# A spectral layer and a gated feed-forward on one core: three first-stage buffers, another order in the opening and on VectorE, half of each table mirrored by GpSimd

## The chip, the core and the metric

The kernel runs on one core of a Trainium2 chip. The core has a matrix engine (TensorE, PE in the profile, with its weight loads as PEld), VectorE (DVE), ScalarE (ACT), GpSimd (POOL) and SyncE (SP), which here issues every DMA. Matrix products land in PSUM, from which VectorE and ScalarE take them; everything else lies in SBUF or in DRAM. The metric is the device time of one execution in microseconds, lower is better. Three executions of the kernel before took 1774.48, 1773.59 and 1771.73 us: median 1773.59 us.

## The reference

```python
# x: 8 x 3136 x 256
X = np.fft.rfft(x, axis=1)
Yr = Xr @ w_r - Xi @ w_i + b_r
Yi = Xr @ w_i + Xi @ w_r + b_i
Yr = np.sign(Yr) * np.maximum(np.abs(Yr) - 0.01, 0.0)   # and Yi in the same way
y = np.fft.irfft(Yr + 1j * Yi, n=3136, axis=1)
h = np.maximum(y @ w_in, 0.0)                            # w_in: 256 x 1024
conv_out = sum(conv_w[k] * (h, shifted by k - 1 rows) for k in range(3))
return (h * sigmoid(conv_out)) @ w_out                   # w_out: 1024 x 256
```

A real Fourier transform along the sequence, a complex 256 × 256 mixing of the features, a soft threshold, the inverse transform, and then a feed-forward layer gated by a convolution of three taps. The feed-forward weights come as float64.

## The kernel before

**The transforms.** 3136 is 49 × 64, and each transform is two rounds of matrix products. Stage one (`stage1`, and `stage1_head` for batch 0) takes 49-point transforms with the constant `f1`; its results go through DRAM (`sc1`), because the second round needs them in another order. Stage two (`stage2`) loads them as `a2` and multiplies them by a table `t2`, one 128 × 128 matrix for each of 25 frequencies `u`. The result is split into a high part `fh` and a low part `fl` for products in the faster fp32r format; `mix` multiplies by the split weights `wmix_hi` and `wmix_lo` with three products in place of four (so there is a difference `d` of real and imaginary part as a third operand), `threshold` applies the soft threshold and splits again (`sh`, `sl`), and `stage3` multiplies by the inverse table, also split (`i1_hi`, `i1_lo`), and stores to DRAM (`sc2`). `stage4`, `up` and `down` are the second half: last round of the inverse transform, and the feed-forward in 28 chunks.

**Items.** Stages two, mixing, threshold and three run over 50 items: eight batches by six groups of four frequencies, and two items that gather the frequency left over. They are software-pipelined in the loop of line 430: in turn `it`, TensorE does stage two of item `it`, mixing of item `it - 1` and stage three of item `it - 3`; the threshold of item `it - 2` runs on ScalarE, VectorE and GpSimd. Between these, stage one of batches 1 to 7 is worked off in halves of a tile (`one`), by a plan of how many are due (`due`, line 434): 2 in turn 0, 3 in turn 1, 4 in turns 2 and 3, 3 in turn 4, later 3 and then 2.6 a turn until they are used up at turn 40. Each half is a product into the single PSUM buffer `ps_s1`, copied by ScalarE to `a1` (two buffers, line 254); each full tile is stored to `sc1`. `load_a2` of a new batch has to wait for all of that batch's stores.

**Order.** In the loop the instruction order of TensorE, VectorE and ScalarE is the order of the program: `some(g, n)` advances a stage by n steps, and the calls of lines 454 to 477 are the hand-written order of one turn. On VectorE that gives, in a turn: difference and low part of the first half of stage two (L306, L307), the threshold (L347, which needs ScalarE's L346 first), two conversion steps, difference and low part of the second half, mixing with bias (L333), the table split (L146, only in early turns), a conversion step, the low part of the difference (L311), and the last additions of the mixing (L337, four of them). ScalarE copies `sh` (L349) right after L347, and GpSimd then makes `sl` (L350), which has one buffer. The conversion steps (`back`, from turn 7) turn the float64 weights into two fp32r parts. SP and GpSimd have no hand-written order; a planner sorts their instructions by readiness, and `tc.issue_after(x)` forbids that what stands in its block is issued ahead of x.

**Tables.** `t2` is loaded in seven slices, slice g holding four frequencies, all 128 rows; the inverse table in seven slices to `raw` buffers (two, shared with the mixing weights), then split by ScalarE and VectorE (`split`, L145 and L146). For all but the frequency left over, rows 64 to 127 of each table are rows 0 to 63 with sine and cosine exchanged and some signs changed.

**The opening** (lines 384 to 418): `f1`, all of batch 0's input, stage one of batch 0 with its eight stores; then, after the last of these, the mixing weights, table slice 0, the first stage-one tile of batch 1 with its two halves, the first `a2`, biases, the second `a2`, two more tiles, and then the loop.

Of the kernel before, what the change touches and what calls it, by code (L numbers as in the profile page):

```python
# [101 lines left out]
def spectral_ffn_kernel(ctx: ExitStack, tc: tile.TileContext, x, w_r, w_i, b_r, b_i,  # L102
# [15 lines left out]
    small = cst.tile([P, 32], F32, name="small")  # L118
    mlam, warm = small[:, 0:1], small[:, 1:2]


    with ExitStack() as ab:
# [28 lines left out]
        def load_t2(g):  # L151
            sl = slice(g * UG, min((g + 1) * UG, U + 1))
            return nc.sync.dma_start(t2[:, sl, :], fwd2v[:, sl, :])

# [16 lines left out]
        def load_inv1(g):  # L171
            sl = slice(g * UG, min((g + 1) * UG, U + 2))
            raw = stg.tile([K2, sl.stop - sl.start, KQ], F32, name="i1_raw", tag="raw", bufs=2)
            nc.sync.dma_start(raw, inv1v[:, sl, :])
            return i1_hi[:, sl, :], i1_lo[:, sl, :], raw
# [76 lines left out]
        def stage1(b, jc, xr):  # L252

            a1 = s1p.tile([K1, JC, D], F32, name="a1", bufs=2)
            for j in range(0, JC, 2):
# [86 lines left out]
        def threshold(v):  # L342
            sh = wk.tile([K2, UG, D], F32R, name="sh")
            sl = wk.tile([K2, UG, D], F32R, name="sl", bufs=1)
            r = wk.tile([K2, UG, D], F32, name="r", bufs=1)
            nc.scalar.activation(r, v, AF.Relu, bias=mlam)  # L346
            nc.vector.scalar_tensor_tensor(v, v, LAM, r, op0=ALU.add, op1=ALU.min)  # L347
            yield sh, sl
            nc.scalar.copy(sh, v)  # L349
            SL_ENG.tensor_tensor(sl, v, sh.bitcast(F32), op=ALU.subtract)  # L350
            yield None
# [21 lines left out]
        nc.vector.memset(mlam, -LAM)  # L373
        nc.vector.memset(warm, 0.0)
        nc.scalar.activation(warm, warm, AF.Sigmoid)

# [8 lines left out]
        with tc.tile_pool(name="hx", bufs=1, reuse_waits="tile") as hx:  # L385
            xh = []
            for p in range(NQ):
                xr, ld = load_x(hx, 0, p, parts=2 if p == 0 else 1, tag=f"hx{p}")
                xh.append(xr)
            with tc.issue_after(ld.ins):  # L390
                st = stage1_head(xh)
        asked = []
# [11 lines left out]
        with tc.issue_after(st.ins):  # L404
            ld = load_mix()
        with tc.issue_after(ld.ins):
            ld = load_t2(0)
        ab.enter_context(tc.manual_schedule(engines={mybir.EngineType.PE}))
        with tc.issue_after(ld.ins):
            ask()  # L410
            some(first, 2)
            a2s[0], ld = load_a2(*items[0])
        with tc.issue_after(ld.ins):
            load_bias()
            a2s[1], ld = load_a2(*items[1])
            for _ in range(2):
                ask()
        ab.enter_context(tc.issue_after(ld.ins))
        wkf, wk, cab, io = [ab.enter_context(tc.tile_pool(name=nm, bufs=n, reuse_waits="tile"))
# [6 lines left out]
        background = later()  # L426
        given, held = 2, []
        xs, vs, ss, i1s = {}, {}, {}, {}
        ab.enter_context(tc.manual_schedule(engines={mybir.EngineType.DVE, mybir.EngineType.Activation}))
        for it in range(n_it + 3):  # L430
# [4 lines left out]
            n_a, given = due - given, due  # L435
            work = 3 if WP0 <= it < n_it else 0

            def one(k=0):
                some(first, n_a > k)
# [6 lines left out]
            if it <= NG:  # L446
                with tc.issue_after(ld.ins) if it + 2 < NG else ExitStack():
# [5 lines left out]
                    i1s[it] = load_inv1(it)  # L453
            some(two, 1)
            th = threshold(vs.pop(it - 2)[0]) if 0 <= it - 2 < n_it else iter(())
            ss[it - 2] = next(th, None)
            back(2)
            some(two, 1)
            some(mx, 8)
            one(1)  # L460
            some(th, 1)
            some(two, 1)
            some(mx, 5)
            if it - 1 in i1s:
                split(*i1s.pop(it - 1))
            back(1)
            some(two, 1)
            some(mx, 5 if n_a > 3 else 9)
            one(2)
            some(mx, 9)  # L470
            one(3)
# [156 lines left out]
```

## Time and profile before

| | |
|---|---|
| the three timed executions, median | 1773.59 us |
| the profiled execution, its own time | 1775.9 us |
| its span, from the first to the last instruction | 1774.1 us |
| mean granted TensorE clock | 0.987 |
| busy: TensorE, weight loads | 1730.7 us (98%), 1608.3 us (91%) |
| busy: VectorE, ScalarE, GpSimd | 1487.7 us (84%), 1209.1 us (68%), 118.5 us (7%) |
| moved by DMA | 165.47 MB |

The profile shows one execution; times in its rows count from the span's start. In a row of a timeline or of groups stand the engine, the line of the kernel, the operation and "tile written <- tiles read" with the shape; "xN" counts instructions that were merged; square brackets give the idle time of the engine before the row and what ended it. Durations of neighbouring instructions overlap on TensorE and, by some 0.1 us, on VectorE, so times from start to start are the better measure of pace. The chain of waits is followed back from the last instruction; its rows give a start, a length and the engine or transfer that held the chain then. "SPq" is SP's queue of DMA issues. PEclk is the granted TensorE clock as a share of full speed, and the DMA share is the mean busy share of the core's 16 DMA engines.

### The profile page before, as it was taken

The page shows a single profiled execution, that of the slowest core. Times are in us where ns is not written, and L with a number is a line of the kernel's source. Part 1 is how long each engine was busy: PE and PEld are TensorE (multiplying, and loading weights), DVE is VectorE, ACT ScalarE, POOL GpSimd, SP SyncE. Part 2 cuts the span into 40 slices and gives each one's busy share as a digit, 9 for nine tenths or more (in the row PEclk, how much of TensorE's full clock was granted, in tenths as well). Part 3 has the DMA queues.
Part 4 walks back from the last instruction along what each step waited for, and adds up shares of the span by engine and source line. Part 5 has one row for each costly group of instructions (what it writes and reads, how often), then busy time and mean ns, then how long its engine had stood idle before and what let it go on. Part 6 is the DMA issues. An engine that isn't in the chain of part 4 may idle for free.

```text
span 1774.1 us, 28820 instructions
## 1 busy us (share of the span) xinstructions
PE 1730.7 (98%) x11872; PEld 1608.3 (91%) x11872; DVE 1487.7 (84%) x1757; ACT 1209.1 (68%) x1565; POOL 118.5 (7%) x54
## 2 busy tenths in 40 slices
PE   6999999999888999999999999999999999999999
PEld 2788888888888999999999999999999999999998
DVE  2778898898994988888888888888888888888887
ACT  2567677677554777777777777777777777777766
POOL 0122222222221000000000000000000000000000
PEclk8999999999988999999999999999999999999999
DMA  8777677666424110111111111111101111100001
GB/s 249 223 236 243 213 230 251 219 224 217 127 93 129 38 40 22 38 46 46 50 48 47 46 40 49 50 40 50 49 21 40 49 50 40 49 22 21 22 21 42
DMA packets 108304, 165.47 MB, mean 93 GB/s; under 512 B 8492, under 2 KB 86316, under 8 KB 108174
## 3 DMA queue, kind: packets, MB, share of 16 engines
q1 hardware_dynamic: 108174, 163.64, 29.1%
q8 instruction: 94, 1.54, 0.3%
q14 instruction: 36, 0.29, 0.0%
HBM read 86.02 MB, written 77.59 MB: 92 GB/s over the span
## 4 chain that ended last, share of the span: by engine, by line
PE 92%; DVE 3%; DMA 3%; issue 1%; ACT 1%; SPq 0%; POOL 0%; ACTq 0%
PE acc L557 31%; PE ps_h L529 31%; PE ps_mx L329 9%; PE ps_s L510 7%; PE ps_s L257 5%; PE ps_s L301 4%; PE ps_s L360 3%; DVE v L337 1%; DMA sc<-a 1%; DMA t<-in_fwd_dram 1%; PE ps_s1h L274 1%; ACT r L346 1%; DMA xr<-in_x_dram 0%; DMA z<-sc 0%; DVE p L333 0%
## 5 line engine op out<-in xcount | busy, mean ns | idle before, releaser
L557 PE MATMUL acc<-wout,gh 128*128 128x256 f32 x3136 | 567.4, 280 | 0.0
L529 PE MATMUL ps_h<-yh,win 128*128 128x450 f32 x1792 | 550.1, 368 | 0.0
L538 DVE SCALAR_TENSOR_TENSOR c<-h,cw,c 128x896 f32<-128x896 f32 x448 | 513.5, 1148 | 38.9 <-ACT c L536 37.3
L557 PEld LDWEIGHTS acc<-wout,gh 128*128 128x128 f32 x3136 | 490.1, 188 | 5.1
L557 PE MATMUL acc<-wout,gl 128*128 128x256 f32 x1568 | 437.4, 280 | 0.0
L531 ACT ACTIVATE h<-ps_h 128x900 f32<-128x900 f32 x224 | 207.4, 926 | 260.4 <-PE ps_h L529 260.4
L529 PEld LDWEIGHTS ps_h<-yh,win 128*128 128x128 f32 x1792 | 339.0, 189 | 26.1 <-DVE yl L517 0.4
L529 PE MATMUL ps_h<-yl,win 128*128 128x450 f32 x896 | 329.4, 368 | 0.0
L544 DVE TENSOR_TENSOR gl<-c,gh 128x896 fp32r<-128x896 f32 x224 | 243.2, 1089 | 76.1 <-ACT gh L543 74.6
L557 PEld LDWEIGHTS acc<-wout,gl 128*128 128x128 f32 x1568 | 293.8, 188 | 0.6
L540 DVE TENSOR_TENSOR c<-h,c 128x896 f32<-128x896 f32 x224 | 243.4, 1087 | 48.1 <-ACT c L539 48.1
L543 ACT CAST gh<-c 128x896 fp32r<-128x896 f32 x224 | 211.1, 943 | 70.3 <-DVE c L540 68.3
L539 ACT ACTIVATE c<-c 128x896 f32<-128x896 f32 x224 | 213.0, 951 | 8.3 <-DVE c L538 4.5
L329 PE MATMUL ps_mx<-wmix_hi,fl 128*128 128x256 f32 x600 | 188.0, 313 | 7.6 <-DVE fl L311 7.6
L329 PE MATMUL ps_mx<-wmix_hi,fh 128*128 128x256 f32 x600 | 185.5, 309 | 1.8 <-DVE p L333 1.5
L529 PEld LDWEIGHTS ps_h<-yl,win 128*128 128x128 f32 x896 | 169.3, 189 | 10.9
L536 ACT ACTIVATE c<-h,cw 128x896 f32<-128x896 f32 x168 | 176.1, 1048 | 2.2 <-DVE gl L544 0.2
L329 PE MATMUL ps_mx<-wmix_lo,fh 128*128 128x256 f32 x600 | 171.1, 285 | 0.0
L350 POOL TENSOR_TENSOR sl<-v,sh 128x1024 fp32r<-128x1024 f32 x50 | 118.3, 2366 | 423.3 <-PE ps_s L360 321.6
L337 DVE TENSOR_TENSOR v<-ps_mx,p 64x512 f32<-64x512 f32 x200 | 137.5, 687 | 7.7 <-PE ps_mx L329 4.8
L329 PEld LDWEIGHTS ps_mx<-wmix_hi,fl 128*128 128x128 f32 x600 | 115.5, 192 | 21.1 <-issue 12.0
L510 PEld LDWEIGHTS ps_s<-i,z 100*128 100x128 f32 x1024 | 130.4, 202 | 4.6 <-DVE yl L517 2.2
(84 smaller groups left out, 1963.6 us busy)
## 6 DMA issues: line engine op xcount, KB each, us to landing
z<-sc SPq DMA_DIRECT2D x64, 400.0 KB
xr<-in_x_dram SPq DMA_DIRECT2D x63, 392.0 KB
a<-sc SPq DMA_DIRECT2D x48, 512.0 KB
sc<-z SPq DMA_DIRECT2D x48, 512.0 KB
out_dram<-o SPq DMA_DIRECT2D x27, 896.0 KB
sc<-a SPq DMA_DIRECT2D x56, 392.0 KB
sc<-ha SPq DMA_DIRECT2D x8, 392.0 KB
win_bits<-in_moe_w_in_dram SPq DMA_DIRECT2D x4, 512.0 KB
```

The source lines that it names most:

```text
L329: nc.tensor.matmul(ps[c][:, k, :], lt, rh, start=(n == 0), stop=(n == len(mm) - 1))
L337: nc.vector.tensor_tensor(v[dst, :, k, :], ps[c][src], p1[src, c], op=ALU.add)
L510: nc.tensor.matmul(ps[:, t, j * K1:(j + 1) * K1], z2[:, j, t * P:(t + 1) * P], i2, start=(j == 0), stop=(j == JG - 1), skip_group_check=True)
L529: nc.tensor.matmul(ps[:, a, 0:CH + 2], lt, rh, start=(n == 0), stop=(n == len(mm) - 1))
L531: nc.scalar.activation(h, ps[:, :, 0:CH + 2], AF.Relu)
L536: nc.scalar.mul(c, h[:, :, 0:CH], cw[:, 0, f:f + 1])
L538: nc.vector.scalar_tensor_tensor(c, h[:, :, k:k + CH], cw[:, k, f:f + 1], c, op0=ALU.mult, op1=ALU.add)
L539: nc.scalar.activation(c, c, AF.Sigmoid)
L540: nc.vector.tensor_tensor(c, h[:, :, 1:CH + 1], c, op=ALU.mult)
L543: nc.scalar.copy(gh, c)
L544: nc.vector.tensor_tensor(gl, c, gh.bitcast(F32), op=ALU.subtract)
L557: nc.tensor.matmul(acc[m // 2][:, m % 2, :], lt[:, sl], rh[:, f, :], start=(f == 0 and n == 0 and m % 2 == 0), stop=(f == NF - 1 and n == ...
```

## The change

Five edits come together.

- `a1`, the stage-one tile, gets three buffers.
- For all but slice 0 of `t2` and the last slice of the inverse table, only rows 0 to 63 are loaded. GpSimd makes rows 64 to 127 from them, by products with a constant +1 or -1 (`mirror_t2`) or with a column of the new tile `sign` that holds +1 or -1 for each group of 32 rows (`load_inv1`): four products for each slice of each table.
- In the opening, the mixing weights and table slice 0 are asked for behind the input of batch 0 and thus ahead of the head's stores; the first `a2` comes right after the last of these stores; the first stage-one tile of batch 1 comes after that `a2`, and its two halves run in turn 0, behind stage two (`given` starts at 0).
- In a turn, both halves of stage two come first; the threshold is cut into three steps, and each comes later: L346 after eight matmuls of the mixing, L347 after L333, `sh` and `sl` after the second stage-one half.
- The conversion steps run from turn 5, still three a turn, spread over the turn.

```diff
-    mlam, warm = small[:, 0:1], small[:, 1:2]
+    mlam, warm, sign = small[:, 0:1], small[:, 1:2], small[:, 2:4]
...
         def load_t2(g):
             sl = slice(g * UG, min((g + 1) * UG, U + 1))
-            return nc.sync.dma_start(t2[:, sl, :], fwd2v[:, sl, :])
+            rows = slice(0, KQ if g == 0 else R2)
+            return nc.sync.dma_start(t2[rows, sl, :], fwd2v[rows, sl, :])
+
+        def mirror_t2(g):
+            top, low = [t2[q, g * UG:(g + 1) * UG, :].rearrange("p u (c h m) -> p c h u m", c=2, h=2) for q in (slice(0, R2), slice(R2, KQ))]
+            for c in range(2):
+                for h in range(2):
+                    nc.gpsimd.tensor_scalar_mul(low[:, c, h], top[:, 1 - c, h], -1.0 if c == h else 1.0)
...
-            nc.sync.dma_start(raw, inv1v[:, sl, :])
+            rows = slice(0, SP if g < NG else K2)
+            nc.sync.dma_start(raw[rows], inv1v[rows, sl, :])
+            if g < NG:
+                top, low = [raw[q].rearrange("p (k o) (m c) -> p o c k m", o=2, c=2) for q in (slice(0, SP), slice(SP, K2))]
+                for o in range(2):
+                    for c in range(2):
+                        nc.gpsimd.tensor_scalar_mul(low[:, o, c], top[:, o, 1 - c], sign[SP:K2, (o + c + 1) % 2:(o + c + 1) % 2 + 1])
...
-            a1 = s1p.tile([K1, JC, D], F32, name="a1", bufs=2)
+            a1 = s1p.tile([K1, JC, D], F32, name="a1", bufs=3)
...
             nc.scalar.activation(r, v, AF.Relu, bias=mlam)
+            yield sh, sl
             nc.vector.scalar_tensor_tensor(v, v, LAM, r, op0=ALU.add, op1=ALU.min)
-            yield sh, sl
+            yield None
...
+        for k in range(4):
+            for c in range(2):
+                nc.vector.memset(sign[k * 32:(k + 1) * 32, c:c + 1], 1.0 if k % 2 == c else -1.0)
...
             with tc.issue_after(ld.ins):
+                load_mix()
+                load_t2(0)
                 st = stage1_head(xh)
...
         with tc.issue_after(st.ins):
-            ld = load_mix()
-        with tc.issue_after(ld.ins):
-            ld = load_t2(0)
-        ab.enter_context(tc.manual_schedule(engines={mybir.EngineType.PE}))
+            a2s[0], ld = load_a2(*items[0])
         with tc.issue_after(ld.ins):
             ask()
-            some(first, 2)
-            a2s[0], ld = load_a2(*items[0])
-        with tc.issue_after(ld.ins):
             load_bias()
             a2s[1], ld = load_a2(*items[1])
             for _ in range(2):
                 ask()
+        ab.enter_context(tc.manual_schedule(engines={mybir.EngineType.PE}))
...
-        given, held = 2, []
+        given, held = 0, []
...
-            work = 3 if WP0 <= it < n_it else 0
+            work = 5 <= it < n_it
...
-            some(two, 1)
+            if 0 < it + 1 < NG:
+                mirror_t2(it + 1)
+            some(two, 2)
             th = threshold(vs.pop(it - 2)[0]) if 0 <= it - 2 < n_it else iter(())
+            some(mx, 8)
+            back(1)
             ss[it - 2] = next(th, None)
-            back(2)
-            some(two, 1)
-            some(mx, 8)
             one(1)
-            some(th, 1)
             some(two, 1)
             some(mx, 5)
             if it - 1 in i1s:
                 split(*i1s.pop(it - 1))
             back(1)
+            some(th, 1)
             some(two, 1)
+            back(1)
             some(mx, 5 if n_a > 3 else 9)
             one(2)
+            some(th, 1)
             some(mx, 9)
             one(3)
             some(mx, 64)
```

## The prediction

> **What bounds the kernel now.** First the busy table by stretches of the span, cut where the work changes: head of stage one, the first items, the repeating middle, the last items, the passage to the second half, the second half.
>
> ```profile
> core 0: us, PE busy (x) PEld busy (x) DVE busy (x) ACT busy (x) POOL busy (x), PEclk, DMA share, GB/s
> 0.00:34.00 34.00, 18.97 (x33) 6.72 (x34) 8.30 (x14) 7.53 (x13) 0.20 (x4) 0.90 0.82 245
> 34.00:62.00 28.00, 22.17 (x123) 16.57 (x122) 18.41 (x29) 14.05 (x27) 2.37 (x1) 0.87 0.97 267
> 62.00:102.00 40.00, 37.72 (x232) 29.96 (x233) 26.71 (x42) 24.02 (x40) 7.07 (x3) 0.92 0.60 191
> 102.00:441.00 339.00, 339.00 (x2424) 291.70 (x2423) 300.83 (x493) 241.50 (x390) 80.76 (x35) 1.00 0.72 231
> 441.00:536.00 95.00, 82.62 (x625) 78.22 (x623) 89.23 (x134) 53.49 (x81) 24.43 (x11) 0.95 0.34 107
> ...
> 569.00:1774.10 1205.10, 1200.83 (x8256) 1156.33 (x8255) 1033.63 (x1033) 855.69 (x1005) 0.00 (x0) 1.00 0.13 40
> ```
>
> Three regimes. From 102 to 441 us and after 569 us TensorE is busy throughout at clock 1.00: a reordering of other engines buys nothing there. From 0 to 102 us TensorE idles, with the DMA engines at 82 to 97% at first. From 441 to 536 us VectorE is the fullest (89.23 of 95), and TensorE waits. The change acts on the second and third regimes alone. Next, the chain of waits of the opening:
>
> ```profile
> 24.10 4.86 DMA sc<-ha
> ...
> 32.37 10.85 DMA t<-in_fwd_dram
> ...
> 43.35 2.02 PE ps_s L301 x16
> ...
> 53.69 8.00 DMA sc<-a
> ...
> 79.98 1.79 PE ps_s L301 x16
> ...
> 101.45 2.02 PE ps_s L301 x16
> ```
>
> The last store of the stage-one head lands at 28.96; item 1 waits for its table slice until 43.22; a store issued at 53.69 holds the chain for 8.00 us. TensorE's and ScalarE's timelines say what that store does:
>
> ```profile
> 4.17 3.70 PE L274 MATMUL ps_s1h<-xr,f 98*98 98x512 f32 x4 [4.17 <-DMA xr<-in_x_dram]
> ...
> 33.72 2.00 PE L257 MATMUL ps_s<-xr,f 98*98 98x512 f32 x2 [10.42 <-DMA xr<-in_x_dram]
> ...
> 38.21 3.35 PE L301 MATMUL ps_s<-t,a 128*128 128x128 f32 x16
> ...
> 52.02 1.95 PE L301 MATMUL ps_s<-t,a 128*128 128x128 f32 x16
> ...
> 61.77 0.59 ACT L258 COPY a<-ps_s 98x512 f32<-98x512 f32 x1 [3.31 <-DMA sc<-a]
> 62.41 2.02 PE L257 MATMUL ps_s<-xr,f 98*98 98x512 f32 x2 [3.79 <-ACT a L258]
> ...
> 68.28 1.92 PE L301 MATMUL ps_s<-t,a 128*128 128x128 f32 x15
> ```
>
> Stage two (L301) of items 0, 1, 2, 3, 4 and 6 starts at 38.21, 43.35, 52.02, 68.28, 79.98 and 101.45. In item 2, ScalarE cannot evict a stage-one half, because both `a1` buffers await their stores; `ps_s1` has one buffer, so TensorE stands 3.79 us and comes back slow (two L257 passes in 2.02 us; 0.86 when warm, below).
>
> For the end of the loop, one item on VectorE, its start-to-start times, and what GpSimd does meanwhile:
>
> ```profile
> 510.47 0.42 DVE L306 TENSOR_TENSOR d<-ps_s,d 128x256 f32<-128x256 f32 x1
> 510.81 0.68 DVE L307 TENSOR_TENSOR fl<-ps_s,fh 128x512 fp32r<-128x512 f32 x1
> 511.66 1.23 DVE L347 SCALAR_TENSOR_TENSOR v<-v,r 128x1024 f32<-128x1024 f32 x1 [0.17 <-ACT r L346]
> 512.80 0.42 DVE L306 TENSOR_TENSOR d<-ps_s,d 128x256 f32<-128x256 f32 x1
> 513.13 0.68 DVE L307 TENSOR_TENSOR fl<-ps_s,fh 128x512 fp32r<-128x512 f32 x1
> 513.73 1.28 DVE L333 TENSOR_TENSOR p<-ps_mx,bias 128x512 f32<-128x512 f32 x2
> 514.92 2.14 DVE L311 TENSOR_TENSOR fl<-d,fh 128x512 fp32r<-128x512 f32 x1
> 516.99 2.80 DVE L337 TENSOR_TENSOR v<-ps_mx,p 64x512 f32<-64x512 f32 x4
> ...
> 519.84 0.42 DVE L306 TENSOR_TENSOR d<-ps_s,d 128x256 f32<-128x256 f32 x1
> ...
> 514.15 2.36 POOL L350 TENSOR_TENSOR sl<-v,sh 128x1024 fp32r<-128x1024 f32 x1 [6.99 <-ACT sh L349]
> ```
>
> An item takes 9.37 us with VectorE never free. L311 lasts 2.14 us; its median over all items is below. It begins behind GpSimd's `sl` (514.15 to 516.51) and ends 0.55 us after it: it is held until GpSimd is done. The Trainium skill, "SBUF — State Buffer", § Who interferes with whom, says that GpSimd and a VectorE instruction with two SBUF inputs exclude each other for a whole instruction; by that rule, the trace agrees (L311 reads `d` and `fh` from SBUF).
>
> **The change, part by part.** More rows, of prices: warm matmuls from the chain, L311's normal size, GpSimd's work, a transposed split held up early, and where the last rows lie.
>
> ```profile
> 155.18 3.27 PE ps_mx L329 x28
> ...
> 440.52 0.86 PE ps_s L257 x2
> L311 DVE TENSOR_TENSOR fl<-d,fh x50: 679/685/2397, 43.6 to 524.3; 128x512 fp32r<-128x512 f32 x50
> L350 POOL TENSOR_TENSOR sl<-v,sh 128x1024 fp32r<-128x1024 f32 x50 | 118.3, 2366 | 423.3 <-PE ps_s L360 321.6 <-ACT sh L349 101.7
> L613 POOL MEMSET const-float32-1.0<- 128x1 f32 x1 | 0.1, 99 | 0.0
> 58.49 1.92 DVE L146 TENSOR_TENSOR i_lo<-i_raw,i_hi 128x512 fp32r<-128x512 f32 x1
> 443.21 0.42 DVE L306 TENSOR_TENSOR d<-ps_s,d 128x256 f32<-128x256 f32 x1 [1.92 <-ACT fh L305]
> ...
> 445.40 0.69 DVE L196 SCALAR_TENSOR_TENSOR wout_e<-wout_bits,wout_e 128x512 int32<-128x512 int32 x1
> ...
> 504.16 0.69 DVE L210 TENSOR_TENSOR wout<-wout_m,wout_rest 128x512 fp32r<-128x512 f32 x1
> ...
> 532.88 2.80 DVE L337 TENSOR_TENSOR v<-ps_mx,p 64x512 f32<-64x512 f32 x4
> ```
>
> *The opening's new order.* SP's queue moves mixing weights and table slice 0 (768 KB) ahead of the head's stores, and the first stage-one tile behind the first `a2` load. The transfers run as a line: between 33.72 and 43.22 landed `a2` 512, biases 256, `a2` 512, two `xr` 784, slice 256: 2320 KB in 9.5 us, 244 KB/us. The head's last store then lands later by 0 (the 768 KB fit into the unused 18%) to 3.1 us (768/244); I take 1, so 30.0. Formerly `xr` and weights moved while that landing was awaited; now the line is empty and starts again. The very first `xr`, 196 KB, serves a matmul at 4.17; less 0.8 of transfer that bounds a start at 3.4 us, SP's own first microsecond included; I take 2. Then `a2` 512, `xr` 392, biases 256, `a2` 512, `xr` 784 and half a slice, 128: 2584 KB, 10.6 us: 42.6. Item 0 starts near 34 instead of 38.21, but its two halves follow it instead of preceding it, so nothing is won by item 1. What was hidden, the weights' five VectorE and three ScalarE instructions, goes between head evictions, where VectorE is busy 8.30 of 34 us; uncovered they cost some 3 us. The eight MEMSETs of `sign` lie under the wait for the first `xr`, until 4.17.
>
> *GpSimd's multiplies.* Four per slice of each table, 64 partitions by 128 elements. No row shows one. From below 0.10 (MEMSET of one element), from above 2.37 (`sl`, 1024 elements, two inputs). I take 0.4: an eighth of `sl` is 0.30, plus the MEMSET's 0.10. Item 1's slice needs its own four, and perhaps the inverse table's four ahead of them: 44.2 to 45.8; **45.0**, 1.65 us later than now. Afterwards both tables' multiplies work one item ahead; queued behind them on GpSimd is `sl`, used an item later, with 6.2 us to spare (an item's 10.0, worked out below, less 1.41 of stage three and 2.37).
>
> *Half tables.* Five slices save 128 KB each, the last 32, six inverse slices 128 each: 1.44 MB, 5.9 us of the line in all. Of this, what lies ahead of the 53.69 store brings it some 4 us earlier; from item 3 on transfers are hidden anyway (share 0.60). Counted inside the next step only.
>
> *Three `a1` buffers.* Item 2's wait goes. An item's work on TensorE: stage two 1.79 (16 matmuls), mixing 36 × 0.117 (3.27/28) = 4.21, a half 0.86, stage three 12 × 0.117 = 1.41. An item with three halves and all stages is thus 10.0. Item 1 keeps its 8.67; item 2, four halves: 9.44 in place of 16.26; item 3, four halves and stage three: 10.85 for 11.70; items 4 and 5 keep 21.47. From 45.0: 53.7, 63.1, 74.0, 95.4 against 101.45. What is late next is item 2's fifth tile, now earlier through the half tables. **Opening: −6 us**; bounds: +3.5 (item 1 at its latest, 3.1 us of stores besides, item 2 gaining 1 us) and −9.
>
> *Middle.* VectorE's sum is unchanged and fits; `sl` starts after stage three as before, beside L337, which reads PSUM. Items 5 and 6 start the weight conversions two items sooner; VectorE's free 1.7 us of an early item (10.0 less 8.3) hide them, and uncovered they cost under 2 us. **0**, ±1.
>
> *VectorE's order at the end.* The differences of both halves come first, then L333, L347, L311, L337; the `sh` copy and `sl` follow L347, so `sl` falls beside L337 instead of L311, and L347 no longer waits for ScalarE. An item: 0.34+0.60+0.33+0.60+1.19+1.14+0.60+2.83 = 7.63 us, TensorE's 7.41 (no halves) below it. Now: 443.21 to 535.68 is 92.5 us for items 41 to 49 and the last mix. Then: 9 × 7.63 = 68.7 us, the last mix's L333, L347, L337 5.2, and conversions. Of these, 14 instructions of some 0.55 us run between 445.40 and 504.77, 7.7 us; the first four fall into items 41 and 42, so a shift by two items leaves ten, 5.5 us. Sum 79.4, that is −13.1. Each new wait between two such nearly equal engines costs something; at 0.2 us an item, **−11**. Bounds: 0 (VectorE then waits for mixing as long as it now waits for GpSimd) and −15, TensorE also keeping its clock (0.95 now).
>
> The sum is −17 us: 1775.9, the profiled execution (span 1774.1 and 1.8 around it), becomes 1758.9. The median of the three runs lies 2.3 below the profiled one: **1756.6 us**.
>
> **Rivals.**
>
> *The multiplies hold VectorE* (17%). While eight of 0.4 us run, 3.2 us an item, instructions with two SBUF inputs stand, as L146 does above (1.92 us; a normal one 0.69). VectorE's early item, 7.63 and 0.69 for the split, becomes 11.5 against TensorE's 10: 1.5 us in five items, 7 in all, which uses up the opening's gain. For it: that row. Against: each multiply is short, and half of VectorE's item reads PSUM. Time: 1773.6 − 11 + 1 = 1764. The rule of the Trainium skill cited above, from "SBUF — State Buffer", speaks for this rival; it gives the same price.
>
> *The end gains nothing* (13%). `sl` starts later within the item; should stage three wait for it, TensorE is late in place of VectorE. Against: it has most of an item to spare. Time: 1773.6 − 6 = 1767.6.
>
> *GpSimd becomes the bound, slower* (9%). In five early items it does eight multiplies and one `sl`. It overruns an item's 10.0 us once a multiply exceeds 0.95 us; the loss, 5 × (8c + 2.37 − 10.0), equals the 17 us won at c = 1.38 us. At `sl`'s own 2.37 us, five items lose 57: 1813 us. For it: nothing here prices so short an instruction, and its operands are strided. Against: GpSimd's idle time, 423 us, and `sl` with eight times the elements.
>
> *It does not do what it says* (6%): the opening stays bound by the line of transfers, `a1` merely waits elsewhere, and the end is limited by TensorE's clock: within 2 us of 1773.6.
>
> **How the numbers follow.** The forecast has 55%. The range runs from 1748 (both gains at their ends, 9 and 15, and the middle's 1) to 1769 (one gain alone, at −6 with 1.4 for the middle), and leaves out the last two rivals and stray ends. A measurement here tells 0.2%, 3.5 us, from no change. Faster: forecast, first two rivals, less some overlap, 82%. Same: the last rival and the first two at their bounds, 9%. Slower: 9%.
>
> **What would show it.** Right: item 3's stage two starts near 63; no ScalarE copy L258 waits for `sc<-a` in item 2; items 42 to 49 follow each other at 8.0 to 8.5 us, with L311 (then further down in the file) at 0.7 and `sl` beside L337; multiplies of 0.3 to 0.5 us. Wrong: multiplies of over 1 us, item 1 after 47, a stage two that waits for GpSimd, L347 or L311 stretched to 2 us, or a middle longer than the present 340 us between item 6 and item 41.

## The result, and the profile after

| | before | after |
|---|---|---|
| median of five executions | 1773.59 us (1771.73 to 1775.54) | 1760.88 us (1759.1 to 1766.73) |
| the profiled execution, its own time | 1775.9 us | 1766.73 us |
| its span | 1774.1 us | 1765.0 us |

The ratio is 0.9932, interval 0.9913 to 0.9951: 12.7 us faster. That lies inside the range and 4 us above the forecast of 1756.6 us. The profiled execution of the changed kernel is the slowest of its five, so its span shows 9.1 us of gain where the medians show 12.7.

First three of the stretches of the span that were shown before, for the changed kernel (start and end, us, busy us and instructions on TensorE, its weight loads, VectorE, ScalarE, GpSimd, then the granted clock, the DMA share and GB/s):

```profile
34.00:62.00 28.00, 18.43 (x92) 14.96 (x93) 10.03 (x17) 8.30 (x18) 11.74 (x20) 0.70 0.98 210
...
102.00:441.00 339.00, 337.34 (x2397) 290.00 (x2396) 294.15 (x490) 239.94 (x388) 82.72 (x35) 0.99 0.72 233
441.00:536.00 95.00, 90.09 (x713) 86.67 (x712) 87.46 (x141) 59.52 (x88) 27.59 (x12) 0.96 0.38 123
```

From 34 to 62 us TensorE does 92 matmuls where it did 123, while the DMA engines are as busy as before (0.98) and move less (210 GB/s for 267). From 441 to 536 us it does 713 for 625. The middle is nearly full (337.34 of 339.00; before, 339.00). So the opening lost and the end won. The chain of waits of the changed kernel, cut to the first 110 us (start, length, what held the chain):

```profile
8.14 12.86 DMA wm_raw<-in_w_i_dram
...
28.36 3.48 DMA sc<-ha
...
35.39 12.09 DMA t<-in_fwd_dram
...
47.57 0.49 POOL t L160
...
48.07 1.52 POOL t L160 x3
...
49.63 3.78 PE ps_s L314 x16
...
66.65 7.54 DMA i_raw<-in_inv_dram
...
76.45 1.77 POOL i_raw L187
...
78.29 2.44 POOL sl L364
...
80.78 1.56 PE ps_s L374 x11
...
104.82 3.18 PE ps_s L314 x16
```

Stage two is L314 now. Item 1 starts at 49.63, behind its slice (landed at 47.48) and the four products that make its lower rows (2.01 us); before it was 43.35, and the forecast 45.0. The chain then goes through a load of the inverse table that lands at 74.19, through its four products, and through `sl`, which stands behind them on GpSimd. Item 6 starts at 104.82, against 101.45 before and 95.4 in the forecast.

Last, one late item of the changed kernel on VectorE (start, us, line, operation):

```profile
506.89 0.42 DVE L319 TENSOR_TENSOR d<-ps_s,d 128x256 f32<-128x256 f32 x1
507.23 0.68 DVE L320 TENSOR_TENSOR fl<-ps_s,fh 128x512 fp32r<-128x512 f32 x1
507.83 0.41 DVE L319 TENSOR_TENSOR d<-ps_s,d 128x256 f32<-128x256 f32 x1
508.16 0.68 DVE L320 TENSOR_TENSOR fl<-ps_s,fh 128x512 fp32r<-128x512 f32 x1
508.76 1.27 DVE L346 TENSOR_TENSOR p<-ps_mx,bias 128x512 f32<-128x512 f32 x2
509.95 1.21 DVE L361 SCALAR_TENSOR_TENSOR v<-v,r 128x1024 f32<-128x1024 f32 x1
511.09 0.68 DVE L324 TENSOR_TENSOR fl<-d,fh 128x512 fp32r<-128x512 f32 x1
511.69 2.81 DVE L350 TENSOR_TENSOR v<-ps_mx,p 64x512 f32<-64x512 f32 x4
...
514.55 0.42 DVE L319 TENSOR_TENSOR d<-ps_s,d 128x256 f32<-128x256 f32 x1
```

The item takes 514.55 - 506.89 = 7.66 us, where the sum said 7.63 and the old order took 9.37. L324, the old L311, is back at 0.68 us, and no row has a wait in brackets.

**Where the 9.1 us of the spans come from.** Start to item 6: +3.4. Item 6 to the first difference of item 41 (448.21): +1.6, of which 1.2 is item 6 itself, 16 matmuls in 3.18 us for 2.02. In a second profile of the change (after2 below) this stretch takes 341.78 us, before it was 341.76, so the 1.6 us belong to the one profile. Item 41 to the end of the last mix: 92.47 before, 79.20 after, -13.3. From there to the first product of the second half: 32.95 before, 30.65 after, -2.3. The second half: +1.5. The sum is -9.1. The -2.3 is no clear gain of the change: in two profiles of one and the same kernel (e_da and e_da2 below) this passage took 32.47 and 30.36 us.

### The profile page after: what moved, and what is told of

It is laid out like the page before. It is cut to its first block, busy times and chain, and to the rows that moved or that the text cites. A ratio compares the mean times of both kernels' runs of the same rounds, so it can differ in the third digit from the quotient of the medians.

```text
span 1765.0 us, 28928 instructions
## 1 busy us (share of the span) xinstructions
PE 1726.8 (98%) x11872; PEld 1606.5 (91%) x11872; DVE 1473.2 (83%) x1765; ACT 1207.1 (68%) x1565; POOL 147.1 (8%) x98
## 3 DMA queue, kind: packets, MB, share of 16 engines
q1 hardware_dynamic: 107406, 162.16, 29.4%
## 4 chain that ended last, share of the span: by engine, by line
PE 93%; DMA 3%; DVE 2%; issue 1%; POOL 0%; ACT 0%; SPq 0%; DVEq 0%; ACTq 0%; POOLq 0%
PE ps_h L546 31%; PE acc L574 31%; PE ps_mx L342 10%; PE ps_s L527 7%; PE ps_s L270 5%; PE ps_s L314 5%; PE ps_s L374 4%; DMA wm_raw<-in_w_i_dram 1%; DMA t<-in_fwd_dram 1%; DVE v L350 0%; DMA i_raw<-in_inv_dram 0%; DMA sc<-a 0%; DMA z<-sc 0%; DMA xr<-in_x_dram 0%; DVE p L346 0%
## 5 line engine op out<-in xcount | busy, mean ns | idle before, releaser
L314 PEld LDWEIGHTS ps_s<-t,a 128*128 128x128 f32 (+1 forms) x800 | 100.5, 199 | 39.9 <-issue 22.0
```

The source lines that it names most:

```text
L314: nc.tensor.matmul(ps[:, k], a2[0:rows, k, t * P:(t + 1) * P], t2[0:rows, u, :], start=(k == 0), stop=(k == UG - 1), skip_group_check=True)
```

## The experiments

The change was taken apart into four parts: **the turn's order** (both halves of stage two first, the threshold in three steps, conversions from turn 5), **the third buffer**, **the opening's order**, and **the halves** (half tables and GpSimd's products). All kernels keep the eight MEMSETs of `sign`. The diffs below are against the kernel named.

| kernel | median us (runs) | ratio to before, interval | stage two of items 1, 3, 4, 6 starts at | item 41 to end of last mix |
|---|---|---|---|---|
| before | 1773.59 (5) | | 43.35, 68.28, 79.82, 101.45 | 92.47 |
| the change | 1760.88 (5) | 0.9932, 0.9913 to 0.9951 | 49.63, 70.41, 83.04, 104.82 | 79.20 |
| e_d | 1758.35 (5) | 0.9904, 0.9884 to 0.9924 | 44.45, 68.58, 79.46, 100.96 | 79.21 |
| e_a | 1770.52 (10) | 0.9982, 0.9968 to 0.9996 | 40.72, 61.02, 72.47, 93.00 | 91.62 |
| e_da | 1753.96 (4) | 0.9886, 0.9867 to 0.9905 | 41.16, 61.22, 72.06, 93.69 | 79.21 |
| e_dao | 1758.61 (4) | 0.9909, 0.9889 to 0.9930 | 45.94, 66.00, 76.87, 98.39 | 79.21 |
| after2 | 1763.71 (6) | 0.9931, 0.9914 to 0.9947 | 48.38, 69.78, 81.36, 102.72 | 79.15 |
| e_dam | 1757.26 (6) | 0.9897, 0.9881 to 0.9913 | 45.61, 66.59, 77.80, 99.72 | 79.15 |
| e_dam_t | 1758.86 (5) | 0.9907, 0.9891 to 0.9922 | 43.27, 63.71, 74.56, 96.35 | 79.15 |
| e_dam_i | 1757.72 (6) | 0.9907, 0.9888 to 0.9927 | 41.99, 61.84, 75.21, 97.15 | 79.14 |
| e_da2 | 1756.18 (4) | 0.9887, 0.9866 to 0.9908 | 42.32, 60.81, 71.66, 93.12 | 79.16 |
| e_split | 1757.30 (4) | 0.9892, 0.9869 to 0.9915 | 45.79, 67.02, 77.87, 99.77 | 79.21 |
| e_late | 1756.88 (4) | 0.9891, 0.9872 to 0.9910 | 43.95, 63.92, 74.79, 96.26 | 79.17 |
| e_t2early | 1750.94 (4) | 0.9862, 0.9839 to 0.9885 | 43.62, 62.45, 73.30, 95.06 | 79.20 |

The kernel before, run beside them, had medians of 1774.54 (e_d to e_dao), 1775.47 (after2 to e_dam_i) and 1775.52 us (e_da2 to e_t2early). So ratios are compared across these groups, and times only inside one.

A caution for the columns of item starts: the stage-one head, which comes before anything that is compared here, ends up to 4 us earlier or later from profile to profile of the same code. In the ten profiles with the old opening its last store was issued between 20.73 (e_a) and 24.77 us (e_t2early); in e_da and e_da2, the same kernel, at 22.08 and 23.29. Where that matters, times are counted from that issue.

### The turn's order alone, and the third buffer alone

e_d has only the turn's order. Against the change it undoes the rest:

```diff
-            rows = slice(0, KQ if g == 0 else R2)
+            rows = slice(0, KQ)
...
-            rows = slice(0, SP if g < NG else K2)
+            rows = slice(0, K2)
...
-            a1 = s1p.tile([K1, JC, D], F32, name="a1", bufs=3)
+            a1 = s1p.tile([K1, JC, D], F32, name="a1", bufs=2)
...
-                load_mix()
-                load_t2(0)
                 st = stage1_head(xh)
...
```

> Only the new order of one turn (threshold in three steps, both halves of stage two first, conversions from turn 5), on the kernel before; two a1 buffers, old opening, whole tables. Theory (the end's gain comes from the order alone, because sl no longer runs beside the low part of the difference): items 41 to the last mix take 79 to 80 us instead of 92.5, stage two of item 6 stays at 101.5, time 1760 us, ratio 0.992 to 0.993. Rival (the gain at the end needs the third buffer or comes from elsewhere): over 86 us there and a time above 1766.

Measured: 1758.35 us, 0.9904, about 16 us faster. Item 41 to the last mix takes 79.21 us, item 6 starts at 100.96, as before. The group of L319, the old L311, over all items of e_d (busy us, mean ns):

```profile
L319 DVE TENSOR_TENSOR fl<-d,fh 128x512 fp32r<-128x512 f32 x50 | 34.2, 685 | 0.1
```

All 50 of them are normal now. The end's gain is real and belongs to this part alone: the rival by which the end gains nothing falls.

e_a has only the third buffer:

```diff
-            a1 = s1p.tile([K1, JC, D], F32, name="a1", bufs=2)
+            a1 = s1p.tile([K1, JC, D], F32, name="a1", bufs=3)
```

> Only the third a1 buffer, on the kernel before. Theory (item 2's wait for the store goes and nothing takes its place): stage two of item 3 starts at 61 to 63 instead of 68.3, item 6 at 95 to 97 instead of 101.45, time 1768 us, ratio 0.9965 to 0.9975. Rival (the halves then wait for their input tiles or the stores behind): item 6 at 100 or later, time within 1.5 us of 1773.6.

Measured: 1770.52 us, 0.9982: a small gain that the interval just separates from none, and less than was expected. TensorE's timeline of e_a, stage two of items 1 to 3:

```profile
40.72 2.84 PE L309 MATMUL ps_s<-t,a 128*128 128x128 f32 x16 [2.19 <-DMA t<-in_fwd_dram]
...
50.98 1.95 PE L309 MATMUL ps_s<-t,a 128*128 128x128 f32 x16
...
61.02 1.95 PE L309 MATMUL ps_s<-t,a 128*128 128x128 f32 x16
```

Item 2 takes 10.04 us in place of 16.26: the wait for the stores of `a1` is gone. From item 1 to item 6 it is 52.28 us against 58.10, 5.8 less; item 6 stands 8.5 us earlier, and the other 2.6 us lie before item 1, where the head of this profile ended early.

### Both together, and the opening's order added

e_da has the turn's order and the third buffer (e_a's line added to e_d).

> New order of a turn and third a1 buffer, old opening, whole tables. Theory (the two gains add, and the opening's new order and the multiplies cost what is missing from the change): 1754 to 1756 us, ratio 0.989 to 0.990, faster than the changed kernel by 5 us; item 6 at 95 to 97. Rival (the opening gains nothing, whatever is done): 1760 us, like the changed kernel.

Measured: 1753.96 us, 0.9886. Run again on another chip as a yardstick (e_da2), it gave 0.9887:

> New order of a turn and three a1 buffers, old opening, whole tables, once more as the reference beside the next three. Expected as before: 1753 to 1757 us, ratio 0.988 to 0.990, item 1 at 41 to 43, item 6 at 93 to 96; q1's share of the 16 engines 29.3%.

Both intervals (0.9866 to 0.9908 together) lie clear of the full change's 0.9913 to 0.9951: **the other two parts cost time**. In us, 1760.88 - 0.9886 x 1773.59 = 7.5.

e_dao adds the opening's order to e_da:

```diff
             with tc.issue_after(ld.ins):
+                load_mix()
+                load_t2(0)
                 st = stage1_head(xh)
...
-            ld = load_mix()
-        with tc.issue_after(ld.ins):
-            ld = load_t2(0)
...
-            ask()
-            some(first, 2)
             a2s[0], ld = load_a2(*items[0])
         with tc.issue_after(ld.ins):
+            ask()
             load_bias()
...
-        given, held = 2, []
+        given, held = 0, []
```

> The changed kernel with whole tables loaded and no multiplies on GpSimd; new opening, three a1 buffers and new order of a turn kept. Theory (the weights' load ahead of the head's stores holds the head up): last head store lands at 31 to 32 as in the changed kernel, item 1 at 46 to 48, item 6 at 98 to 101, time 1758 us, ratio 0.991. Rival (the multiplies alone spoil the opening): item 1 at 43 to 44, item 6 at 94 to 96, time 1754 us or less.

Measured: 1758.61 us, 4.7 us above e_da beside it, and item 6 at 98.39 for 93.69, 4.7 us later. The intervals of the two ratios overlap, so the time alone doesn't settle it; the item starts agree with it. The chain of e_dao, from the head's last store to item 1:

```profile
26.10 4.65 DMA sc<-ha
...
34.33 11.47 DMA t<-in_fwd_dram
...
45.94 3.54 PE ps_s L309 x16
```

and of e_da:

```profile
22.08 3.78 DMA sc<-ha
...
29.69 11.34 DMA t<-in_fwd_dram
```

Item 1's slice lands 15.05 us after the head's last store has landed (45.80 less 30.75), in e_da 15.17 us (41.03 less 25.86). So moving 768 KB out of this stretch shortened it by nothing. The line was less full instead: while the head's last store was under way, the DMA share was 0.58 in e_dao and 0.88 in e_da, and from its landing to that of the slice 0.83 and 1.05 (packets count where they start, so a short stretch can show more than 1). And the head's last store comes later: it is issued at 26.10, after that of every profile with the old opening. Why, ScalarE's timeline of the changed kernel shows, with SP's longest waits from 20 to 60 us below it (us in total, times, longest):

```profile
15.27 0.59 ACT L291 COPY ha<-ps_s1h 98x512 f32<-98x512 f32 x1 [1.13 <-PE ps_s1h L287]
21.03 0.62 ACT L145 CAST wmix_hi<-wm_raw 128x512 fp32r<-128x512 f32 x1 [5.17 <-DMA wm_raw<-in_w_i_dram]
21.55 0.58 ACT L291 COPY ha<-ps_s1h 98x512 f32<-98x512 f32 x1
```

```profile
SPq L292 <- DVE ha L289: 9.3, 4, 5.1
SPq L299 <- DMA sc<-ha: 3.2, 1, 3.2
```

ScalarE takes the split of the weights ahead of a head eviction, and stands 5.17 us for their load to land at 21.00. The eviction waits behind it, TensorE waits for the eviction, and SP waits for the half that it is to store. In e_dao ScalarE's wait is 3.23 us.

### The split of the weights behind the head

e_late is e_dao with the split behind all of the head's evictions, and ScalarE and VectorE follow the program's order in the head (`split_mix` holds the lines of `load_mix` that make the split):

```diff
...
-                load_mix()
+                wm_raw = load_mix()
                 load_t2(0)
-                st = stage1_head(xh)
+                with tc.manual_schedule(engines={mybir.EngineType.DVE, mybir.EngineType.Activation}):
+                    st = stage1_head(xh)
+                    split_mix(wm_raw)
```

> The changed kernel with whole tables and no multiplies, and with ScalarE's and VectorE's weight split written behind all head evictions; the load stays where the change puts it. Theory (the split, waiting for its load, stood ahead of evictions and held the head up): no 5 us of ScalarE idle in the head, last head store issued at 24 to 25 instead of 26 to 28, item 1 at 42.5 to 44.5, item 6 at 95 to 97, time 1755 to 1757 against 1758.6 with the split ahead. Rival (the emptied line of transfers behind the head's last store costs the most): item 1 at 45 or later, time 1758 or more.

Measured: 1756.88 us, 0.9891. ScalarE's timeline of e_late, and its chain:

```profile
20.25 0.59 ACT L288 COPY ha<-ps_s1h 98x512 f32<-98x512 f32 x1 [1.13 <-PE ps_s1h L284]
21.96 0.59 ACT L288 COPY ha<-ps_s1h 98x512 f32<-98x512 f32 x1 [1.13 <-PE ps_s1h L284]
22.45 0.62 ACT L145 CAST wmix_hi<-wm_raw 128x512 fp32r<-128x512 f32 x1
```

```profile
23.58 5.25 DMA sc<-ha
...
33.01 10.81 DMA t<-in_fwd_dram
```

The evictions run at TensorE's pace, the head's last store is issued 2.5 us earlier than in e_dao, and item 6 starts 2.1 us earlier (96.26). So the hold-up is real: without it the last issue, at 23.58, is back among those of the old opening. Of the 4.7 us that item 6 was late in e_dao it accounts for 2.1 in these profiles, and 2.6 to 3.1 us against e_da and e_da2 stay. As heads differ by as much from profile to profile, this division is rough. In time the step can't be told (0.9891 against 0.9909, intervals overlapping).

### The halves, together and one table at a time

e_dam is e_da with the halves, in the old opening:

```diff
-            rows = slice(0, KQ)
+            rows = slice(0, KQ if g == 0 else R2)
...
-            rows = slice(0, K2)
+            rows = slice(0, SP if g < NG else K2)
             nc.sync.dma_start(raw[rows], inv1v[rows, sl, :])
+            if g < NG:
+                top, low = [raw[q].rearrange("p (k o) (m c) -> p o c k m", o=2, c=2) for q in (slice(0, SP), slice(SP, K2))]
+                for o in range(2):
+                    for c in range(2):
+                        nc.gpsimd.tensor_scalar_mul(low[:, o, c], top[:, o, 1 - c], sign[SP:K2, (o + c + 1) % 2:(o + c + 1) % 2 + 1])
...
+            if 0 < it + 1 < NG:
+                mirror_t2(it + 1)
```

> New order of a turn, three a1 buffers and half tables with multiplies, but the old opening. Against the same kernel with whole tables (1754.0 us; items 1, 4 and 6 at 41.2, 72.1 and 93.7). Theory (the multiplies cost more than the half loads save: item 1 waits for them, and sl stands behind multiplies that wait for their table): item 1 at 43 to 46, item 4 another 1.5 to 2.5 us later, item 6 at 96 to 99, time 1756 to 1758. Rival (the multiplies are harmless, only the new opening spoils it): item 6 at 92 to 94, time 1752 to 1754.

Beside it ran the full change once more, as a control (after2, no edit), and the two tables alone:

> The changed kernel once more, as a control beside the next three, and for a second profile of its opening (the first one came from the slowest of its five executions). Theory: 1759 to 1761 us; the pattern is the same as in the first profile: ScalarE and VectorE idle some 3 to 5 us in the head until the weights have landed, item 1 waits for GpSimd's multiplies, stage three of item 0 waits for sl; item 6 at 100 to 104, items 41 to the last mix 79.2 us. Rival (the first profile was an accident): no such waits, item 6 at 95 to 97.

e_dam_t halves only `t2`, so the inverse table's lines above are taken out again:

```diff
-            rows = slice(0, SP if g < NG else K2)
+            rows = slice(0, K2)
             nc.sync.dma_start(raw[rows], inv1v[rows, sl, :])
-            if g < NG:
...
```

> As the kernel with new order, three buffers, half tables and old opening, but only the stage-two table is halved; the inverse table is loaded whole. Theory (each table has its own wait): item 1 at 42.5 to 44, turns 2 to 5 as long as with whole tables (10.2, 9.8, 10.8, 10.0), item 6 at 95 to 96, time 1755 us. Rival (GpSimd's multiplies hold VectorE by sharing its path to SBUF): every turn with multiplies is 0.5 us or more longer.

e_dam_i halves only the inverse table:

```diff
-            rows = slice(0, KQ if g == 0 else R2)
+            rows = slice(0, KQ)
...
-            if 0 < it + 1 < NG:
-                mirror_t2(it + 1)
```

> As the kernel with new order, three buffers, half tables and old opening, but only the inverse table is halved; the stage-two table is loaded whole. Theory: item 1 at 40.5 to 41.5 as with whole tables, then turn 3 longer by 1 to 2 us, because sl of item 0 or 1 stands behind multiplies that wait for the inverse slice; item 6 at 94.5 to 96, time 1755 us. Rival (the cost comes from the stage-two table alone): turn 3 at 10.8 us, item 6 at 93.7 or earlier, time 1753.5 or less.

Measured: after2 repeats the change (0.9931). e_dam is at 0.9897, e_dam_t and e_dam_i at 0.9907; e_da was 0.9886 and 0.9887. All intervals overlap, so the halves cost at most some us of time. In the profile the cost is seen: counted from the head's last issue, item 6 starts 75.8 us later in e_dam (99.72 less 23.88), and 71.6 and 69.8 in e_da and e_da2. Of this, 2.7 us lie before item 1 (21.7 us after that issue, 19.1 and 19.0 in e_da and e_da2). GpSimd's rows name two ways, first in the changed kernel:

```profile
47.57 2.01 POOL L160 TENSOR_SCALAR t<-t 64x128 f32<-64x128 f32 x4 [47.13 <-DMA t<-in_fwd_dram]
49.68 2.70 POOL L187 TENSOR_SCALAR i_raw<-i_raw,small 64x128 f32<-64x128 f32 x4
...
74.34 3.87 POOL L187 TENSOR_SCALAR i_raw<-i_raw,small 64x128 f32<-64x128 f32 x4 [1.63 <-DMA i_raw<-in_inv_dram]
78.29 2.43 POOL L364 TENSOR_TENSOR sl<-v,sh 128x1024 fp32r<-128x1024 f32 x1
```

Then in e_dam_i:

```profile
66.52 3.96 POOL L187 TENSOR_SCALAR i_raw<-i_raw,small 64x128 f32<-64x128 f32 x4 [3.79 <-DMA i_raw<-in_inv_dram]
70.56 2.34 POOL L364 TENSOR_TENSOR sl<-v,sh 128x1024 fp32r<-128x1024 f32 x1
```

and in e_dam_t:

```profile
62.38 2.36 POOL L359 TENSOR_TENSOR sl<-v,sh 128x1024 fp32r<-128x1024 f32 x1 [2.86 <-issue]
```

A product of `t2` takes 0.50 us, one of the inverse table 0.68 (2.70 / 4). In the row of 3.87 us the last of the four takes 1.76 us by itself, from 76.45 on, beside VectorE's L361 (76.58 to 77.79), which reads `v` and `r` from SBUF; one in e_dam_i (1.77 us) and one in e_dam (1.89) lie beside L361 in the same way. The four of `t2` stand ahead of item 1. The four of the inverse table stand, from item 3's turn on, waiting for their load, with the first `sl` behind them, and stage three of that turn behind `sl`. In e_dam_i that turn, item 3 to item 4, is 13.37 us long; in e_dam_t, where `sl` stands behind no such product, 10.85, as in e_da (10.84). How much the second way costs varies: with both tables halved the turn takes 12.63 us in the change, 11.58 in after2 and 11.21 in e_dam.

### Whole slices in two transfers

The halves save 1.44 MB of loads, yet item 1's slice took 12.09 us from issue to landing in the change, and a whole one 11.34 in e_da. e_split asks what a transfer of 64 rows costs. It is e_da with each slice loaded whole, in two transfers of 64 rows:

```diff
-            return nc.sync.dma_start(t2[rows, sl, :], fwd2v[rows, sl, :])
+            for rows in (slice(0, R2), slice(R2, KQ)):
+                ld = nc.sync.dma_start(t2[rows, sl, :], fwd2v[rows, sl, :])
+            return ld
...
-            nc.sync.dma_start(raw[rows], inv1v[rows, sl, :])
+            for rows in (slice(0, SP), slice(SP, K2)):
+                nc.sync.dma_start(raw[rows], inv1v[rows, sl, :])
```

> As the reference, but every slice of both tables is loaded whole by two transfers of 64 rows. Same bytes, 14 more transfers. Theory (a transfer to 64 partitions keeps the DMA engines as long as one to all 128 with twice the bytes, so that half slices saved nothing): each of some 12 slices costs the line another 1 us, q1's share rises by 0.6 to 0.8 points to about 30%, item 1 1 to 2 us later than in the reference, time 3 to 8 us more. Rival (bytes decide): share 29.3 to 29.4%, item 1 within 0.7 us, time within 2 us.

Measured: 1757.30 us, 0.9892; e_da2 beside it 1756.18. From 34 to 62 us, in the stretches of e_da2:

```profile
34.00:62.00 28.00, 25.62 (x149) 19.46 (x148) 18.39 (x31) 14.98 (x29) 2.36 (x1) 0.89 0.98 269
```

of e_split:

```profile
34.00:62.00 28.00, 23.19 (x114) 18.19 (x115) 13.42 (x24) 12.33 (x25) 0.00 (x0) 0.75 0.97 232
```

and of e_dam:

```profile
34.00:62.00 28.00, 23.08 (x116) 17.89 (x115) 13.66 (x24) 12.54 (x25) 14.70 (x28) 0.76 0.97 224
```

The engines are as busy in all three, and with the tables in pieces of 64 rows they move 232 and 224 GB/s for 269. Item 1 starts 21.5 us after the head's last issue (24.27) in e_split, 19.0 in e_da2: 2.5 us later for the same bytes, of which about 1 us passes before slice 1 is asked for (9.7 us after that issue, 8.7 in e_da2). That e_split has 14 transfers more can't be the whole reason, since e_dam has as many as e_da and moves less still.

The trace also records every packet. Those of 2048 bytes, of which the table slices consist, take 103 ns on average from 34 to 62 us in e_da2, 106 in e_da, 138 in e_split and 159 in e_dam; those of 1024 bytes take 56, 56, 66 and 64. So a transfer of 64 rows is slower for its bytes. By these means half a slice takes 0.5 x 159 / 105 = 0.76 of a whole one's packet time, an estimate.

Neither expectation came true as a whole: item 1 moved as the theory has it, but the time hardly did (1.1 us), and the share of the transfers' time over the whole span neither (29.4% for 29.3%), as the rival has it.

The Trainium skill, "SBUF — State Buffer", § Door 1: The DMA port swizzle, says that partitions 0 to 63 reach only 8 of the 16 ports, and gives 196 GB/s for them against 328 for all 128, in transfers of 1 MiB. An estimate from these figures of the page: a half slice then takes 0.5 x 328 / 196 = 0.84 of a whole slice's time. e_split agrees in direction, and the packets of e_dam come to the 0.76 above; no run here measures a transfer by itself.

### Slice 1 asked for earlier

Since item 1 waits for its slice in the kernels above, e_dam_i apart, e_t2early, which is e_da, asks for slice 1 together with slice 0:

```diff
-            ld = load_t2(0)
+            load_t2(0)
+            ld = load_t2(1)
...
-                    if it + 3 <= NG:
+                    if it and it + 3 <= NG:
                         load_t2(it + 1)
```

> As the reference, but table slice 1 is asked for together with slice 0, in the time in which the line waits for the head's last store, instead of behind two stage-one tiles. Theory (item 1 waits only for its slice): item 1 2.5 to 3.5 us earlier than in the reference, items 2 and 3 then wait for stage-one tiles and give back 1 to 2; item 6 1 to 2.5 us earlier, time 1751.5 to 1753.5. Rival (the line as a whole limits the opening up to item 3): item 6 as in the reference, time within 1 us of it.

Measured: 1750.94 us, 0.9862, the fastest of all; its interval lies clear of the change's, not of e_da's. Stage two of item 1 on TensorE's timeline of e_t2early:

```profile
43.62 2.34 PE L309 MATMUL ps_s<-t,a 128*128 128x128 f32 x16 [0.89 <-ACT fh L313]
```

and its chain:

```profile
47.29 6.71 DMA a<-sc
...
54.06 7.42 DMA sc<-a
```

Item 1 no longer waits for the slice, but it starts hardly earlier, 18.9 us after the head's last issue (24.77) for 19.0 in e_da2: it waits for the eviction of item 0, which comes behind two stage-one halves. And item 6, counted from that issue, starts 70.3 us later, between e_da2's 69.8 and e_da's 71.6. Other transfers of the same line hold the chain instead: as a whole it is no shorter, only in another order. That e_t2early is faster than the kernel before and than the change is shown; that this last step has a part in it is not: in the profiles, most of what it has ahead of e_da2 lies in the passage to the second half (27.96 us for 30.36), which differs by 2.1 us between e_da and e_da2.

## Why the prediction came out as it did

The range and the sign held, the forecast was 4 us low. Its two large terms missed in opposite directions, so that the total came so near is in part luck.

**VectorE's order at the end: right, and too cautious.** The pure sum was 79.4 us; every kernel with this order took 79.1 to 79.2. The 0.2 us that was held back for new waits in each item was not needed, so the term is -13.3 and not -11. As forecast, L324 is at 0.7 us and `sl` lies beside the additions that read PSUM.

**Third buffer: right.** Item 2's wait for `a1` is gone in e_a, and no eviction waits for a store of `a1` in the change. From item 1 to item 6 this is worth 5.8 us in the profile and some 4 us of time, with 0.7 to 5.7 as its interval. That item 3 starts at 70.41 and not near 63 is what was added in front of it.

**The opening: wrong.** Forecast -6, profile +3.4 (after2: +1.3). Step by step the 9.4 us between 95.4 and 104.82 are:

| step, as the prediction put it | forecast | measured | late by |
|---|---|---|---|
| landing of the head's last store | 30.0 | 31.84 | 1.8 |
| from there to the landing of slice 1 | 12.6 | 15.64 | 3.0 |
| from there to item 1 | 2.4 | 2.15 | -0.2 |
| item 1 to item 2 | 8.67 | 10.86 | 2.2 |
| item 2 to item 3 | 9.44 | 9.92 | 0.5 |
| item 3 to item 4 | 10.85 | 12.63 | 1.8 |
| item 4 to item 6 | 21.47 | 21.78 | 0.3 |

The prediction took 79.98, where the chain of before enters item 4, for that item's start; the timeline has 79.82. The last row of its sum should thus have been 21.63.

- *The head.* The step that failed is "goes between head evictions". In the change a cast on ScalarE waits 5.17 us for its load, and the evictions behind it wait too. The prediction priced the split's work (some 3 us if uncovered), not its wait. e_late shows the hold-up by taking it away.
- *The line.* The line "244 KB/us" and "2 us" for the restart were mis-sized for what moves then: 12.6 us were forecast from the head's landing to that of slice 1, and 15.64 measured. In the new order, e_dao's slice lands 15.05 us after the head, with 768 KB less to move than in the old order, where it takes 14.3 to 15.7 us: the old order had used the wait for the head's landing for the weights, and the new one leaves the line half empty there (DMA share 0.88 in e_da, 0.58 in e_dao, 0.50 in the change). The half slice gave nothing either (15.64 us in the change), and e_split shows why in part: transfers of 64 rows move at a lower pace. That the half empty line is what cancels the 768 KB is argued from these shares, not tested.
- *Item 1 to item 2.* Nearly all of it is the clock: TensorE stands 6.63 us before item 1, and the 16 matmuls then take 3.78 us at a granted clock of 0.50, instead of the 2.02 of before at 1.00. The forecast had kept the old 8.67; e_da, where TensorE stands 3.15 us, takes 10.23.
- *Item 3 to item 4.* "With 6.2 us to spare" is what failed. That the products take 0.50 and 0.68 us instead of 0.4 matters little; that they wait for a transfer with `sl` behind them, and that one of them stands beside L361, does. e_dam_i shows the long turn, e_dam_t shows it gone.

**Middle: nearly right.** 0 was forecast; TensorE is busy for 337.34 of the 339 us from 102 to 441, and the 1.6 us that were lost between item 6 and item 41 are mostly one cold stage two, which after2 does not have.

**The rivals.** *The multiplies hold VectorE*: this hardly happened. L146 and L324 are stretched by some 0.1 us beside the products in the change (0.78 us for 0.68), and once to 2.06 us in e_dam, beside `sl`. It went rather the other way: L361 keeps its 1.21 us, and the product beside it takes 1.76. *GpSimd becomes the bound*: not as a sum, since eight products and `sl` are about 4 x 0.50 + 4 x 0.68 + 2.37 = 7.1 us of a turn of 10; but its queue did delay stage three, through a wait. *The end gains nothing*: falls with e_d. *It does not do what it says*: true of the opening, in which the line of transfers still sets the pace, and not of the end.

## What to carry to other kernels

Before a load-dependent instruction is moved ahead of others, look at what stands behind it on its engine and at when its load lands; its own length is the smaller price. Count a transfer saved only if a row shows that half of it lands earlier: rows of one half of the partitions saved bytes here and no time. Where one engine is the fullest, its start-to-start times added up gave the new item to 0.03 us, even with TensorE at 7.41 us close to VectorE's 7.63.

## What the runs showed of the hardware

- The pace of a full line of transfers depends on how its tables are cut: 269 GB/s with transfers of 128 rows, 232 GB/s with the same tables in pieces of 64 rows, at a DMA share of 0.98 and 0.97. A packet of 2048 bytes took 103 to 106 ns on average in whole slices, 138 and 159 ns in such pieces.
- A GpSimd product of 64 x 128 elements takes 0.50 us with a constant factor and 0.68 us with a factor for each row and another stride; one beside a VectorE instruction of 1.21 us with two inputs in SBUF took 1.76 us.
- The same 16 matmuls of stage two take 1.95 us at a granted clock of 1.00, and 3.78 us at 0.50 after a wait of 6.63 us, so a wait for a transfer can cost TensorE more than its length. The last wait alone does not tell the clock: after 1.78 us they took 2.02 us (before), after 1.43 us 3.38 us (e_dam_i).
